# Three of four score products of a batch placed directly ahead of packed weights, in the up-projection's PSUM banks, and the second softmax done by halves of heads

## The chip, the core and the metric

The kernel runs on one core of one Trainium2 chip. The time is that of one execution in device microseconds (us). The core's engines work side by side, each through its own list of instructions in order, and wait for each other by semaphores. PE multiplies matrices (PEld is its weight load), DVE and ACT do the elementwise work and empty PSUM, POOL does a little, and SP, ACT and POOL issue DMAs. PE writes its results to PSUM, eight banks of 128 x 512 float32.

## The reference, cut to what matters

```python
def sm_attn(qq, kk, vv):                      # softmax(qq kk^T / 8) vv
    s = scale * np.matmul(qq, kk.transpose(0, 1, 3, 2))
    a = np.exp(s - np.max(s, axis=-1, keepdims=True))
    return np.matmul(a / (np.sum(a, axis=-1, keepdims=True) + 1e-09), vv)
p_packed = sm_attn(p, k, v)                   # p: (8, 8, 32, 64); q, k, v: (8, 8, 576, 64)
attn = sm_attn(q, p_packed, p_packed)         # first and second softmax
x = attn.transpose(0, 2, 1, 3).reshape(8 * 576, 512)
h = x @ w_in                                  # 512 -> 2048
out = (h * np.tanh(np.log1p(np.exp(h)))) @ w_out   # mish, 2048 -> 512
```

For each of 8 batches and 8 heads, 32 learned queries `p` gather the keys and values (first softmax), then the 576 rows of `q` read those 32 packed values (second softmax). The result goes through a two-layer network with mish between.

## The kernel before

The value product of the second attention and `w_in` are joined: for each batch the packed values of the heads are multiplied with `w_in` ("packed weights", `packed_w`, 512 of the 2048 columns at a time, chunks 0 to 3), and the second softmax's weights, turned so that heads and packs stand on the partitions (`aT_hi`, `aT_lo`), are multiplied with them. Both products of the network are done in three matmuls each, from a high and a low part of each operand.

The main loop has one step `t` for each of 8 x 16 groups; group `f` of batch `b` is 128 of the 2048 columns. A step issues on PE, in the order of the code: `down(dn, 0)`, `up(0)`, `down(dn, 1)`, `down(dn, 2)`, `up(1)`, `down(dn, 3)`. `up(0)` and `up(1)` are six matmuls each (256 and 320 columns) that write PSUM bank `ps_h0` (`ps_h` number 90 in lists) and `ps_h1` (91); ACT's mish then empties that bank (`mish`, lines 806 and 808), so `up` of the next step has to wait for it. `down(dn, c)` is three matmuls of 512 columns for one of four row chunks, of the group two steps back; `halves` (817, 818) makes its operands on DVE. Two more PSUM banks (`ps_a`) serve everything else.

Meanwhile the attention of batch `b + 1` is done in pieces between these matmuls: the generator `attention` is advanced twice a step by `advance`. It turns keys and queries on DVE (`lanes`, 450), and makes four small products on PE, by `products`: `score(0)` and `score(1)` (first softmax, heads 0 to 3 and 4 to 7) and `match(0)` and `match(1)` (second softmax). Each is eight matmuls on a quarter-wide piece of the array (64 rows by 32 columns of it, "64*32" in rows), into the two `ps_a` banks. What empties the banks is kept in `pending` and issued by `flush`: `spread` (478 to 482) after a score, `blocks` (568) after a match. `packed_w` is eight matmuls in the same 64*32 form, at the end of steps f = 2, 6, 10 and 14. The second softmax runs on both halves of the heads at once: `peak` (297, 298) on DVE, `rise` (304, the exponential) on ACT, `share`, `back`, then `upper` and `lower` make `aT_hi` and `aT_lo`.

The exponential and mish need different tables on ACT, so an exponential is preceded and followed by an ACT_TABLE_LOAD. PE's order is that of the code. On DVE and ACT a scheduler of the language sets the order of the main loop's instructions when the program is built.

Of the kernel before, what the change touches and what calls it, by code (L numbers as in the profile page):

```python
# [8 lines left out]
F32 = mybir.dt.float32  # L9
# [12 lines left out]
WB = 4  # L22
WARM = (10, 2, 3, 6, 6)
OB = 2
ATTENTION = {0: 4, 1: 0}
LOAD0 = 0
LOADS = {0: 1, 2: 1, 4: 1, 5: 1, 6: 1}
LATER = 12
# [3 lines left out]
TOGETHER = 2  # L32
# [9 lines left out]
def body(  # L42
# [12 lines left out]
    B, H, S, D = q.shape  # L55
    NP = p.shape[2]
    DF = w_in.shape[1]
    DO = w_out.shape[1]
    P = 128
# [5 lines left out]
    NF = DF // P  # L65
    HALF = S // 2
# [7 lines left out]
    att = ctx.enter_context(tc.tile_pool(name="att", bufs=2))  # L74
# [65 lines left out]
    def psum(pool, shape, name):  # L140
        return pool.tile(shape, F32, name=name, tag="acc" if pool is ps_acc else "ps_a")
# [31 lines left out]
    class Batch:  # L173
# [35 lines left out]
        def score(self, g):  # L209
            self.s_ps = scores(ps_a, self.pT[:, g, :], self.kT)  # L210
            mx = stat.tile([P, 2], F32, name="mx")
            for u in range(2):
                nc.vector.reduce_max(out=mx[:, u:u + 1], in_=self.s_ps[u], axis=AX.X)
            self.top = stat.tile([P, 1], F32, name="top")
            nc.vector.tensor_scalar(
                out=self.top, in0=mx[:, 0:1], scalar1=mx[:, 1:2], scalar2=-scale, op0=ALU.max, op1=ALU.mult
            )
# [64 lines left out]
        def match(self, g, pool):  # L282

            s2 = scores(pool, self.ppT[:, g, :], self.qT[g])
            if g == 0:
                self.a2 = moe.tile([P, 2, S // NP, NP], F32, name="a2", tag="aT_hi")
            a2f = self.a2[:, g].rearrange("a g n -> a (g n)")
            for u in range(2):
                nc.vector.transpose(out=a2f[:, u * HALF:(u + 1) * HALF], in_=s2[u])
            yield  # L290
# [84 lines left out]
    class Later(Batch):  # L375
# [78 lines left out]
                self.pinned(x)  # L454
            return t

        def products(self, packT, xT, g, paired):
            ps = [psum(ps_a, [P, HALF], f"ps_s{u}") for u in range(2)]
            for u in range(2):
                for h in range(4):  # L460
                    n = (h ^ g if paired else h) * NP
                    nc.tensor.matmul(  # L462
                        out=ps[u][h * NP:(h + 1) * NP, :],
                        lhsT=packT[u * D:(u + 1) * D, n:n + NP],
                        rhs=xT[u * D:(u + 1) * D, h ^ g, :],
                        start=True, stop=True,
                        tile_position=(u * D, h * NP),
                    )
            return ps

        def score(self, g):
            s_ps = self.products(self.pT[:, g, :], self.kT[g], g, True)
            pending.append(lambda: self.spread(g, s_ps))

        def spread(self, g, s_ps):
# [82 lines left out]
            nc.tensor.transpose(out=ps, in_=self.pp[g].rearrange("a u d -> a (u d)"), identity=ident)  # L558
            pending.append(lambda: nc.vector.tensor_copy(out=self.ppT[:, g, :], in_=ps))

        def match(self, g):
            s2 = self.products(self.ppT[:, g, :], self.qT[g], g, False)
            pending.append(lambda: self.blocks(g, s2))

        def blocks(self, g, s2):
# [2 lines left out]
                nc.vector.transpose(out=a2f[:, u * HALF:(u + 1) * HALF], in_=s2[u])  # L568

        def attention(self):  # L570


            self.by = "ACT" if self.b == 1 else None
            self.start()
            self.kT, self.qT = {}, {}
            for g in range(2):
                self.kT[g] = self.lanes(self.k_t[g])
                load_next()
                yield
            if self.b == 2:  # L580
                yield
                yield
            if self.b < TOGETHER:
                for g in range(2):
                    self.score(g)
                    yield
                    flush()
                    yield
                self.exps()
                for g in range(2):  # L590
                    self.qT[g] = self.lanes(self.q_t[g])
                    load_next()
                    yield
            else:
                self.score(0)
                yield
                flush()
                yield
                self.qT[0] = self.lanes(self.q_t[0], True)
                load_next()  # L600
                yield
                self.score(1)
                yield
                flush()
                self.qT[1] = self.lanes(self.q_t[1], True)
                load_next()
                yield
                self.exps()
                yield
                yield  # L610
            yield from self.turn_weights()
            self.sums(self.exped)
            yield
            if self.b >= TOGETHER:
                yield
                yield
            else:
                for g in range(2):
                    self.values(g)
                    yield  # L620
            for g in range(2):
                self.turned(g)
            yield
            self.a2 = att.tile([P, 2, S // NP, NP], F32, name="a2", tag="a", bufs=1)
            for g in range(2):
                self.match(g)
                yield
                flush()
                yield
            both = slice(0, 2)  # L630
            self.peak(both)
            yield
            self.rise(both)
            yield
            self.share(both)
            for g in range(2):
                self.back(g)
                yield
                self.upper(g)
                yield  # L640
                self.lower(g)

        def columns(self, a):

# [90 lines left out]
            nc.vector.tensor_tensor(out=lo[:, g], in0=ps[g], in1=hi[:, g].bitcast(F32), op=ALU.subtract)  # L735
        return [(hi[:, g], lo[:, g]) for g in range(2)]

    def packed_w(b, c):

        ps = [ps_a.tile([P, FC], F32, name=f"ps_w{g}", tag="ps_a") for g in range(2)]  # L740
        for h in range(4):
            for g in range(2):
                weave(b, ps[g].rearrange("p (u x) -> p u x", u=2), wi[c][g][:, :, h // 2], g, h)
        return [part(x) for x in ps]

    whole = {}
# [135 lines left out]
    def flush():  # L882
        while pending:
            pending.pop(0)()

    def advance(gen):
        flush()
        next(gen, None)

    def finish(gen):  # L890
        flush()
        for _ in gen:
            flush()
# [3 lines left out]
    def load_next():  # L897
        if owed["t"] < LATER and len(to_load) <= 6 * (B - 2):
            owed["n"] += 1
        elif to_load:  # L900
            b, x, g = to_load.pop(0)
            batches[b].load(x, g)
# [47 lines left out]
    with tc.manual_schedule(engines={mybir.EngineType.PE}):  # L950
# [51 lines left out]
        first.rise(slice(1, 2))  # L1002
        groups = []
        gen = iter(())
        g_rest = None
        for t in range(n_groups + LAG):
            b, f = divmod(t, NF)
            grp = None
            if t < n_groups:
                if f == 0:  # L1010
                    if b % 2 == 0:
                        g_rest = ([], [])
                if f == ATTENTION.get(b, 1) and b + 1 < B:
                    gen = batches[b + 1].attention()
                if t == LOAD0:
                    opening.close()
                    kv.append(ctx.enter_context(tc.tile_pool(name="kv", bufs=2, side="left", reuse_waits="tile")))
                owed["t"] = t
                for _ in range(LOADS.get(t, 0)):
                    load_next()  # L1020
                if t >= LATER and owed["n"]:
                    owed["n"] -= 1
                    load_next()
                if t == 1:
                    grp = ahead
                else:
                    grp = Group(b, f, None if t == 2 else wps[b, f // 4 if b else f // 2], g_rest)
                    grp.tiles()
                if t == 0:
                    ahead = Group(0, 1, wps[0, 0], g_rest)  # L1030
                    ahead.tiles()
# [24 lines left out]
                join(3)  # L1056
            if dn:
                down(dn, 0)
            if 2 < t < FLOATS:
                grp.up_floats((0,), (0, 1))  # L1060
                first.upper(t - 2)
            elif grp and t > NF:
                grp.up(0)
            if chunk:
                flush()
            else:
                advance(gen)
# [22 lines left out]
                down_rest(dn)  # L1090
            if dn:
                down(dn, 2)
            if t:
                advance(gen)
            if 2 <= t < FLOATS:
                if t == 2:
# [13 lines left out]
            if last:  # L1110
                flush()
                down_rest(dn)
            if dn:
                down(dn, 3)
            if grp and f % 4 == 2 and (b or f == NF - 2):
                nb, nch = divmod(b * (NF // 4) + f // 4 + 1, NF // 4)
                if nb < B:
                    flush()
                    if nb > b:
                        finish(gen)  # L1120
                    if f == NF // 4 + 2 and TOGETHER <= b + 1 < B:
                        batches[b + 1].both_values()
                    wps[nb, nch] = packed_w(nb, nch)
            elif b == 0 and not chunk:
                advance(gen)
# [29 lines left out]
```

## Time and profile before

| | before |
|---|---|
| median of 3 runs | 736.9 us (736.84 to 737.53) |
| span of the profiled execution | 735.2 us, 12658 instructions |
| PE busy | 724.3 us (99%) |
| DVE busy | 424.9 us (58%) |
| ACT busy | 296.6 us (40%) |
| POOL busy | 71.1 us (10%) |
| granted TensorE clock, mean | 0.999 |

The span runs from the first to the last instruction; the median of the runs is 1.7 us above it. Busy shares are means over the whole run; which wait ends last at a place is read from the rows.

### The profile page before, as it was taken

The page shows a single profiled execution, that of the slowest core. Times are in us where ns is not written, and L with a number is a line of the kernel's source. Part 1 is how long each engine was busy: PE and PEld are TensorE (multiplying, and loading weights), DVE is VectorE, ACT ScalarE, POOL GpSimd, SP SyncE. Part 2 cuts the span into 40 slices and gives each one's busy share as a digit, 9 for nine tenths or more (in the row PEclk, how much of TensorE's full clock was granted, in tenths as well). Part 3 has the DMA queues.
Part 4 walks back from the last instruction along what each step waited for, and adds up shares of the span by engine and source line. Part 5 has one row for each costly group of instructions (what it writes and reads, how often), then busy time and mean ns, then how long its engine had stood idle before and what let it go on. Part 6 is the DMA issues. An engine that isn't in the chain of part 4 may idle for free.

```text
span 735.2 us, 12658 instructions
## 1 busy us (share of the span) xinstructions
PE 724.3 (99%) x5094; PEld 553.9 (75%) x5094; DVE 424.9 (58%) x727; ACT 296.6 (40%) x692; POOL 71.1 (10%) x103
## 2 busy tenths in 40 slices
PE   9899999999999999999999999999999999999997
PEld 5455655787887878787887878877788788888885
DVE  4899887848647374546735566373833637342322
ACT  4777655534434233242522424343423424232221
POOL 1585540000000000000000000000000000000000
PEclk9999999999999999999999999999999999999999
DMA  9999972454002630144202460125101000010002
GB/s 239 297 291 231 304 121 54 94 90 96 1 37 57 116 65 1 58 73 99 33 0 72 73 121 10 44 45 100 33 1 44 30 1 1 1 58 1 1 0 72
DMA packets 187114, 56.34 MB, mean 77 GB/s; under 512 B 175024, under 2 KB 177328, under 8 KB 187056
## 3 DMA queue, kind: packets, MB, share of 16 engines
q1 hardware_dynamic: 183376, 47.14, 29.0%
q10 hardware_dynamic: 2336, 4.20, 1.5%
q0 software_dynamic: 1344, 4.20, 1.5%
q8 instruction: 40, 0.66, 0.4%
q14 instruction: 18, 0.15, 0.1%
HBM read 46.07 MB, written 9.44 MB: 75 GB/s over the span
## 4 chain that ended last, share of the span: by engine, by line
PE 92%; DVE 4%; ACT 2%; DMA 1%; issue 0%; POOL 0%; SPq 0%; DVEq 0%; ACTq 0%
PE ps_h L784 25%; PE acc L822 15%; PE acc L824 14%; PE acc L823 14%; PE acc L842 5%; PE ps_w L702 5%; PE ps_s L462 2%; PE ps_rest L824 2%; PE ps_rest L823 2%; PE ps_rest L822 2%; PE ps_h L531 1%; PE ps_h L796 1%; DMA q_n<-in_q_dram 1%; PE ps_a L511 1%; PE ps_h L909 1%; PE ps_kq L155 1%
## 5 line engine op out<-in xcount | busy, mean ns | idle before, releaser
L806 ACT ACTIVATE g<-ps_h 128x256 f32<-128x256 f32 (+2 forms) x256 | 97.0, 384 | 300.6 <-PE ps_h L784 280.4
L822 PE MATMUL acc<-wo_hi,g_hi 128*128 128x512 f32 x448 | 181.2, 405 | 0.0
L824 PE MATMUL acc<-wo_hi,g_lo 128*128 128x512 f32 x448 | 177.1, 395 | 0.0
L823 PE MATMUL acc<-wo_lo,g_hi 128*128 128x512 f32 x448 | 176.7, 394 | 0.0
L784 PE MATMUL ps_h<-aT_hi,wp_hi 128*128 128x256 f32 x496 | 153.0, 308 | 0.4 <-ACT g L806 0.4
L817 DVE CAST g_hi<-g 128x512 fp32r<-128x512 f32 x112 | 47.4, 423 | 183.4 <-ACT g L806 183.1
L784 PE MATMUL ps_h<-aT_lo,wp_hi 128*128 128x256 f32 x496 | 146.4, 295 | 0.2 <-DVE aT_lo L342 0.2
L784 PE MATMUL ps_h<-aT_hi,wp_lo 128*128 128x256 f32 x496 | 146.2, 295 | 0.0
L822 PEld LDWEIGHTS acc<-wo_hi,g_hi 128*128 128x128 f32 x448 | 84.2, 188 | 40.3 <-issue 21.3
L784 PEld LDWEIGHTS ps_h<-aT_hi,wp_hi 128*128 128x128 f32 x496 | 93.4, 188 | 15.5 <-issue 5.9
L784 PEld LDWEIGHTS ps_h<-aT_lo,wp_hi 128*128 128x128 f32 x496 | 93.4, 188 | 12.5 <-issue 3.3
L824 PEld LDWEIGHTS acc<-wo_hi,g_lo 128*128 128x128 f32 x448 | 84.1, 188 | 21.5 <-DVE g_lo L818 2.0
L784 PEld LDWEIGHTS ps_h<-aT_hi,wp_lo 128*128 128x128 f32 x496 | 93.4, 188 | 0.0
L823 PEld LDWEIGHTS acc<-wo_lo,g_hi 128*128 128x128 f32 x448 | 84.1, 188 | 9.2
L818 DVE TENSOR_TENSOR g_lo<-g,g_hi 128x512 fp32r<-128x512 f32 x112 | 77.2, 689 | 6.5 <-DVE g_hi L817 0.5
L842 PE MATMUL acc<-wo,g 128*128 128x512 f32 x128 | 61.3, 604 | 0.0
L714 DVE TENSOR_TENSOR wp_lo<-ps_w,wp_hi 128x512 fp32r<-128x512 f32 x56 | 36.1, 683 | 18.5 <-ACT wp_hi L713 18.5
L713 ACT CAST wp_hi<-ps_w 128x512 fp32r<-128x512 f32 x56 | 30.1, 591 | 37.4 <-PE ps_w L702 37.4
L851 POOL DMA_DIRECT2D out_dram<-o x16 | 9.2, 576 | 318.9 <-DVE o L831 314.7
L702 PE MATMUL ps_w<-wi,ppT 64*32 64x512 f32 (+1 forms) x576 | 37.6, 553 | 2.1 <-DVE wi L688 1.2
L842 PEld LDWEIGHTS acc<-wo,g 128*128 128x128 f32 x128 | 22.4, 189 | 22.8 <-issue 19.2
L808 ACT ACTIVATE g_rest<-ps_h 128x64 f32<-128x64 f32 x128 | 28.2, 220 | 0.0
(128 smaller groups left out, 752.0 us busy)
## 6 DMA issues: line engine op xcount, KB each, us to landing
w_st<-in_moe_w_in_dram SPq DMA_DIRECT2D x16, 512.0 KB, 8.0
w_st<-in_moe_w_out_dram SPq DMA_DIRECT2D x16, 512.0 KB, 7.4
q_n<-in_q_dram SPq DMA_DIRECT2D x56, 144.0 KB, 3.1
v_n<-in_v_dram SPq DMA_DIRECT2D x56, 128.0 KB, 2.8
k_n<-in_k_dram SPq DMA_DIRECT2D x32, 144.0 KB, 3.3
out_dram<-o ACTq DMA_DIRECT2D x14, 256.0 KB, 2.0
k_n<-in_k_dram SPq DMA_DIRECT2D x96, 32.0 KB, 2.0
out_dram<-o POOLq DMA_DIRECT2D x12, 256.0 KB, 2.4
```

Of the source, the lines that this page charges most:

```text
L702: nc.tensor.matmul(out=ps[h * NP:(h + 1) * NP, :], lhsT=ppTb[row:row + D, g, h * NP:(h + 1) * NP], rhs=w[row:row + D], start=True, stop=Tr ...
L713: nc.scalar.copy(out=hi, in_=ps)
L714: nc.vector.tensor_tensor(out=lo, in0=ps, in1=hi.bitcast(F32), op=ALU.subtract)
L784: nc.tensor.matmul(out=ps, lhsT=w[:, fs], rhs=a[:, g, cs], start=(n == 0), stop=(n == 5))
L806: nc.scalar.activation(out=self.act[:, a:a + m], in_=ps[:, :m], func=AF.Mish)
L808: nc.scalar.activation(out=self.g_rest[self.b % 2][self.f // 4][:, self.f % 4, :], in_=ps[:, m:n], func=AF.Mish)
L817: nc.vector.tensor_copy(out=hi, in_=self.act)
L818: nc.vector.tensor_tensor(out=lo, in0=self.act, in1=hi.bitcast(F32), op=ALU.subtract)
L822: nc.tensor.matmul(out=acc, lhsT=hi[:, cs], rhs=wh, start=start, stop=False)
L823: nc.tensor.matmul(out=acc, lhsT=hi[:, cs], rhs=wl, start=False, stop=False)
L824: nc.tensor.matmul(out=acc, lhsT=lo[:, cs], rhs=wh, start=False, stop=stop)
L842: nc.tensor.matmul(out=accs[c], lhsT=grp.act[:, cs], rhs=wo[f], start=f == 0, stop=f == NF - 1)
```

## The change

Nothing changes for the attention of batch 1. For batches 2 to 7 the generator is replaced by a table, `plan`, which says what is issued at which half step (`step(2 * f)` and `step(2 * f + 1)`), and three of the four small products move to the loop's own code, in `excursion`:

- at f = 2, `score(0)` of the next batch stands right ahead of `packed_w(b, 1)`; at f = 8, `match(0)` right ahead of `packed_w(b, 3)`; at f = 12, `match(1)` right ahead of `packed_w(b + 1, 0)`. They write `ps_h0` and `ps_h1` instead of `ps_a`. `score(1)` stays alone, at f = 3, in `ps_a`; `packed_w(b, 2)` stays at the end of f = 6;
- at these three steps `up(0)` moves behind `down(dn, 2)`, and `down(dn, 3)` ahead of `up(1)`;
- the second softmax runs in two halves, each after its match: `peak`, `rise`, `share`, `back`, `upper`, `lower` from f = 8 on for heads 0 to 3, from f = 12 on for heads 4 to 7.

```diff
-ATTENTION = {0: 4, 1: 0}
+ATTENTION = {0: 4}
+SOFTEN = (17, 25)
+SCORE_0, MATCH_0, MATCH_1 = 2, 8, 12
...
-        def products(self, packT, xT, g, paired):
-            ps = [psum(ps_a, [P, HALF], f"ps_s{u}") for u in range(2)]
+        def products(self, packT, xT, g, paired, beside=False):
+            if beside:
+                ps = [up_ps[u][:, :HALF] for u in range(2)]
+            else:
+                ps = [psum(ps_a, [P, HALF], f"ps_s{u}") for u in range(2)]
...
+        def plan(self):
...
+            first = 0 if self.b == TOGETHER else 2
+            steps = {
+                first: [self.start, lambda: self.keys(0)],
+                first + 1: [lambda: self.keys(1)],
+                4: [lambda: self.queries(0)],
+                7: [lambda: self.score(1)],
+                8: [lambda: self.queries(1)],
+                9: [self.exps],
+                11: [lambda: [None for _ in self.turn_weights()]],
+                12: [lambda: self.sums(self.exped)],
+                15: [lambda: self.turned(0), lambda: self.turned(1)],
+            }
+            for g, n in enumerate(SOFTEN):
+                gs = slice(g, g + 1)
+                steps[n] = [lambda gs=gs: self.peak(gs)]
+                steps[n + 1] = [lambda gs=gs: self.rise(gs)]
+                steps[n + 2] = [lambda gs=gs: self.share(gs)]
+                steps[n + 3] = [lambda g=g: self.back(g), lambda g=g: self.upper(g)]
+                steps[n + 4] = [lambda g=g: self.lower(g)]
+            return steps
...
-    def packed_w(b, c):
+    def packed_w(b, c, before=None):
+        if before:
+            before()
         ps = [ps_a.tile([P, FC], F32, name=f"ps_w{g}", tag="ps_a") for g in range(2)]
         for h in range(4):
             for g in range(2):
                 weave(b, ps[g].rearrange("p (u x) -> p u x", u=2), wi[c][g][:, :, h // 2], g, h)
+        if before:
+            flush()
         return [part(x) for x in ps]
...
+    def excursion(b, f):
+        n = batches[b + 1]
+        if f == SCORE_0:
+            wps[b, 1] = packed_w(b, 1, lambda: n.score(0, True))
+        elif f == MATCH_0:
+            wps[b, 3] = packed_w(b, 3, lambda: n.match(0, True))
+        else:
+            wps[b + 1, 0] = packed_w(b + 1, 0, lambda: n.match(1, True))
...
             if dn:
                 down(dn, 0)
+            away = grp and TOGETHER <= b + 1 < B and f in (SCORE_0, MATCH_0, MATCH_1)
+            if away:
+                flush()
+                excursion(b, f)
...
-            elif grp and t > NF:
+            elif grp and t > NF and not away:
                 grp.up(0)
...
             if dn:
                 down(dn, 2)
+            if away:
+                grp.up(0)
+                down(dn, 3)
...
-            if dn:
+            if dn and not away:
                 down(dn, 3)
```

How the built programs stand at the places of the second softmax, in the attention of batch 5 (`a_4604` is its tile of scores). On PE before, `match(1)` stood alone between `up(0)` and a `down`:

```order
L784 MATMUL ps_h_90<-aT_hi,wp_lo 128x256
L462 MATMUL ps_s_4649<-xT,ppT 32x288 x4
L462 MATMUL ps_s_4650<-xT,ppT 32x288 x4
L822 MATMUL acc_4216<-wo_hi_1917,g_hi 128x512
L823 MATMUL acc_4216<-wo_lo_1918,g_hi 128x512
```

and in the changed kernel, at f = 12, it stands between a `down` and the packed weights (lines are those of the changed file; 467 is the product, 714 the packed weights, 840 a `down`):

```order
L840 MATMUL acc_4224<-wo_hi,g_lo 128x512
L467 MATMUL ps_h_90<-xT,ppT 32x288 x4
L467 MATMUL ps_h_91<-xT,ppT 32x288 x4
L714 MATMUL ps_w_4783<-wi_0_92,ppT 32x512
L714 MATMUL ps_w_4784<-wi_1_93,ppT 32x512
```

So the product and the packed weights follow each other without a matmul of the whole array between them; `up(0)` of this step comes six `down` matmuls later.

On ACT before, the one exponential of the second softmax and its two table loads stood between the mish of `up(0)` and that of `up(1)` of one step:

```order
L806 ACTIVATE g<-ps_h_90 128x256
L304 ACT_TABLE_LOAD
L304 ACTIVATE a_4604<-a_4604 128x1152
L806 ACT_TABLE_LOAD
L806 ACTIVATE g<-ps_h_91 128x256
```

In the changed kernel the exponential of a half stands behind the casts of the packed weights and ahead of the mish of `up(0)` of its own step (306 is the exponential, 725 the cast, 822 mish):

```order
L725 CAST wp_hi<-ps_w_4783 128x512
L725 CAST wp_hi<-ps_w_4784 128x512
L306 ACT_TABLE_LOAD
L306 ACTIVATE a_4604<-a_4604 128x576
L822 ACT_TABLE_LOAD
L822 ACTIVATE g<-ps_h_90 128x256
L822 ACTIVATE g<-ps_h_91 128x256
```

So the emptying of `ps_h0` comes behind an exponential and a table load. What the exponential waits for stands on DVE in this order in the changed kernel (575 is `blocks`, 452 the next batch's keys, 299 and 300 `peak`, 726 the low part of the packed weights):

```order
L575 STREAM_TRANSPOSE a_4604<-ps_h_90 128x288
L575 STREAM_TRANSPOSE a_4604<-ps_h_91 128x288
L452 STREAM_TRANSPOSE xT<-k_n 128x1152
L299 TENSOR_REDUCE mx_4819<-a_4604 128x18
L300 TENSOR_TENSOR a_4604<-a_4604,mx_4819 128x576
L726 TENSOR_TENSOR wp_lo<-ps_w_4783,wp_hi 128x512
```

The keys of the following batch stand between `blocks` and `peak`, as they did before. These orders are the same at f = 8 and f = 12 for the attention of batches 3 to 6; for batch 7 the keys are missing (there is no batch 8), and for batch 2 the mish of `up(0)` stands ahead of the exponential, that of `up(1)` behind it. On SP and POOL the two programs have the same rows in the same order.

## Rows read from the trace of the kernel before

**Rows 1.** The page: busy us, share of the span, instructions.

```profile
PE 724.3 (99%) x5094; PEld 553.9 (75%) x5094; DVE 424.9 (58%) x727; ACT 296.6 (40%) x692; POOL 71.1 (10%) x103
```

**Rows 2.** Waits of PE: us in total, times, longest us.

```profile
PE ps_h L784 <- ACT g L806: 0.4, 1, 0.4
```

**Rows 3.** Timeline of PE, batch 2: start us, us, engine, line, operation, tiles, shape.

```profile
304.25 0.28 PE L784 MATMUL ps_h<-aT_lo,wp_hi 128*128 128x256 f32 x1
304.37 0.28 PE L784 MATMUL ps_h<-aT_hi,wp_lo 128*128 128x256 f32 x1
304.57 0.71 PE L462 MATMUL ps_s<-xT,pT 64*32 64x288 f32 x16
305.22 0.50 PE L822 MATMUL acc<-wo_hi,g_hi 128*128 128x512 f32 x1
305.56 0.40 PE L823 MATMUL acc<-wo_lo,g_hi 128*128 128x512 f32 x1
305.80 0.40 PE L824 MATMUL acc<-wo_hi,g_lo 128*128 128x512 f32 x1
...
308.41 1.09 PE L702 MATMUL ps_w<-wi,ppT 64*32 64x512 f32 x16
...
309.77 0.39 PE L823 MATMUL acc<-wo_lo,g_hi 128*128 128x512 f32 x1
...
314.04 0.40 PE L822 MATMUL acc<-wo_hi,g_hi 128*128 128x512 f32 x1
...
318.41 0.40 PE L822 MATMUL acc<-wo_hi,g_hi 128*128 128x512 f32 x1
```

**Rows 4.** Timeline of PE, opening: one 64*32 product alone, then two in sequence.

```profile
27.81 0.64 PE L702 MATMUL ps_w<-wi,ppT 64*32 64x256 f32 x8 [1.20 <-DVE wi L688]
...
37.84 1.03 PE L702 MATMUL ps_w<-wi,ppT 64*32 64x256 f32 x16
```

**Rows 5.** Timeline, all engines, around `match(1)` of the attention of batch 5.

```profile
434.78 0.72 PE L462 MATMUL ps_s<-xT,ppT 64*32 64x288 f32 x16
...
435.53 0.85 DVE L568 STREAM_TRANSPOSE a<-ps_s 128x288 f32<-128x288 f32 x2 [1.17 <-PE ps_s L462]
...
436.31 1.33 DVE L450 STREAM_TRANSPOSE xT<-k_n 128x1152 f32<-128x1152 f32 x1
...
437.56 1.31 DVE L297 TENSOR_REDUCE mx<-a 128x36 f32<-128x1152 f32 x1
```

**Rows 6.** Groups by line and shape: count | busy us, mean ns | idle before.

```profile
L713 ACT CAST wp_hi<-ps_w 128x512 fp32r<-128x512 f32 x56 | 30.1, 591 | 37.4 <-PE ps_w L702 37.4
...
L304 ACT ACT_TABLE_LOAD x7 | 9.0, 1283 | 0.1
...
L298 DVE TENSOR_TENSOR a<-a,mx 128x576 f32<-128x576 f32 x2 | 1.5, 768 | 0.1
...
L297 DVE TENSOR_REDUCE mx<-a 128x18 f32<-128x576 f32 x2 | 1.4, 722 | 0.0
L304 ACT ACTIVATE a<-a 128x576 f32<-128x576 f32 x2 | 1.4, 684 | 0.5 <-DVE a L298 0.5
```

**Rows 7.** Timeline, all engines, batch 1: mish after an exponential, and PE.

```profile
146.36 0.40 PE L824 MATMUL acc<-wo_hi,g_lo 128*128 128x512 f32 x1
146.67 0.66 ACT L806 ACTIVATE g<-ps_h 128x256 f32<-128x256 f32 x2
147.11 0.19 PEld L784 LDWEIGHTS ps_h<-aT_hi,wp_hi 128*128 128x128 f32 x1 [0.78 <-ACT g L806]
147.11 0.38 PE L784 MATMUL ps_h<-aT_hi,wp_hi 128*128 128x256 f32 x1 [0.35 <-ACT g L806]
...
147.33 0.28 PE L784 MATMUL ps_h<-aT_lo,wp_hi 128*128 128x256 f32 x1
```

**Rows 8.** Timeline of DVE: `spread` after a `score(0)` (batch 5).

```profile
397.29 0.82 DVE L478 TENSOR_REDUCE mx<-ps_s 128x1 f32<-128x288 f32 x2 [1.36 <-PE ps_s L462]
...
398.34 0.94 DVE L482 TENSOR_SCALAR a<-ps_s,top 128x288 f32<-128x288 f32 x2
```

More of the change, by code (lines that the diff above doesn't have):

```diff
@@ L469, in products, with score @@
             return ps
-        def score(self, g):
-            s_ps = self.products(self.pT[:, g, :], self.kT[g], g, True)
+        def score(self, g, beside=False):
+            s_ps = self.products(self.pT[:, g, :], self.kT[g], g, True, beside)
             pending.append(lambda: self.spread(g, s_ps))
@@ L559, in turned, with match @@
             pending.append(lambda: nc.vector.tensor_copy(out=self.ppT[:, g, :], in_=ps))
-        def match(self, g):
-            s2 = self.products(self.ppT[:, g, :], self.qT[g], g, False)
+        def match(self, g, beside=False):
+            if g == 0:
+                self.a2 = att.tile([P, 2, S // NP, NP], F32, name="a2", tag="a", bufs=1)
+            s2 = self.products(self.ppT[:, g, :], self.qT[g], g, False, beside)
             pending.append(lambda: self.blocks(g, s2))
@@ L570, in attention @@
         def attention(self):
-            self.by = "ACT" if self.b == 1 else None
+            self.by = "ACT"
             self.start()
@@ L579, in attention @@
                 yield
[L580 to L595, printed above, removed]
+            for g in range(2):
+                self.score(g)
                 yield
@@ L598, in attention @@
                 yield
-                self.qT[0] = self.lanes(self.q_t[0], True)
+            self.exps()
+            for g in range(2):
+                self.qT[g] = self.lanes(self.q_t[g])
                 load_next()
[L601 to L609, printed above, removed]
                 yield
@@ L613, in attention @@
             yield
-            if self.b >= TOGETHER:
+            for g in range(2):
+                self.values(g)
                 yield
[L616 to L620, printed above, removed]
             for g in range(2):
@@ L623, in attention @@
             yield
-            self.a2 = att.tile([P, 2, S // NP, NP], F32, name="a2", tag="a", bufs=1)
             for g in range(2):
@@ L641, in attention, with keys, queries @@
                 self.lower(g)
+        def plan(self):
+            self.by = None
+            self.kT, self.qT = {}, {}
+            first = 0 if self.b == TOGETHER else 2
[18 more added lines that the diff above has]
+            return steps
+        def keys(self, g):
+            self.kT[g] = self.lanes(self.k_t[g])
+            load_next()
+        def queries(self, g):
+            self.qT[g] = self.lanes(self.q_t[g], True)
+            load_next()
         def columns(self, a):
@@ L888, in advance, with step @@
         next(gen, None)
+    def step(n):
+        flush()
+        for x in steps.pop(n, ()):
+            x()
+    def excursion(b, f):
[6 more added lines that the diff above has]
+            wps[b + 1, 0] = packed_w(b + 1, 0, lambda: n.match(1, True))
     def finish(gen):
@@ L1004, in body @@
         gen = iter(())
+        steps = {}
         g_rest = None
@@ L1012, in body @@
                         g_rest = ([], [])
-                if f == ATTENTION.get(b, 1) and b + 1 < B:
+                if f == ATTENTION.get(b):
                     gen = batches[b + 1].attention()
+                if f == 0 and TOGETHER <= b + 1 < B:
+                    steps = batches[b + 1].plan()
                 if t == LOAD0:
@@ L1058, in body @@
                 down(dn, 0)
+            away = grp and TOGETHER <= b + 1 < B and f in (SCORE_0, MATCH_0, MATCH_1)
+            if away:
+                flush()
+                excursion(b, f)
             if 2 < t < FLOATS:
@@ L1061, in body @@
                 first.upper(t - 2)
-            elif grp and t > NF:
+            elif grp and t > NF and not away:
                 grp.up(0)
-            if chunk:
+            if b:
+                step(2 * f)
+            elif chunk:
                 flush()
@@ L1092, in body @@
                 down(dn, 2)
-            if t:
+            if away:
+                grp.up(0)
+                down(dn, 3)
+            if b:
+                step(2 * f + 1)
+            elif t:
                 advance(gen)
@@ L1116, in body @@
                 nb, nch = divmod(b * (NF // 4) + f // 4 + 1, NF // 4)
-                if nb < B:
+                if nb < B and (nb, nch) not in wps:
                     flush()
-                    if nb > b:
+                    if nb > b == 0:
                         finish(gen)
```

## The prediction

> **What bounds the kernel now.** The page comes first: PE is busy in 724.3 of 735.2 us, DVE in 58% and ACT in 40% [rows 1]. The waits say whether PE's share hides stalls: in the main loop PE waits for ACT once, for 0.4 us, before an `up` [rows 2]. So the time is what PE has to issue, and a change gains by shortening PE's own list or loses by making it wait. The timeline of PE shows what its list holds besides full matmuls. The reader should look at starts, since the ends overlap: an `up` matmul follows the one before by 0.12 us, a `down` matmul by 0.24 (305.56 to 305.80), and a whole step without extras, from one `down` matmul to the same place a step on, takes 4.37 us (314.04 to 318.41) [rows 3]. Around the small 64*32 products this rhythm breaks. The profiled execution spans 735.2 us and the median of the runs is 736.9, so 1.7 us lie around the span; the sum below is a difference and goes onto the median. About 0.2%, 1.5 us, is what a measurement of this kernel can tell from no change.
>
> **What the change removes on PE.** A `score` or `match` that stands alone starts 0.20 us after the last `up` matmul (304.37 to 304.57), 0.08 more than the rhythm; the second full matmul behind it starts 0.99 us after the product did; the first one behind it needs 0.34 to its successor (305.22 to 305.56) instead of 0.24 [rows 3]. The packed weights show the same with 512 columns for 288: 1.36 us (308.41 to 309.77) [rows 3]. The difference of 0.37 for 224 columns is 1.65 ns a column, so the 288 columns of a product cost 0.48 us and the rest of the 0.99, less the 0.24 that a `down` takes anyway, is 0.27 of fixed cost; with the 0.08 at the entry 0.35 us. Behind each other in the same form the fixed cost should be paid once. Rows for that exist in the opening: one product of 256 columns lasts 0.64, two in sequence 1.03, so the second adds 0.39, no more than its columns (0.42) [rows 4]. Bounds for one joined pair: 0.18 (only the gap at the entry and the 0.10 of the first full matmul fall away) to 0.35. I take 0.31, near the upper end because of the opening. The Trainium skill's TensorEngine Tiling, section Key Properties, says that changing the tiling mode, not just the tile, drains the engine; the gaps on either side of the 64*32 work in these rows agree with it. There are three pairs for each of six batches: 18 x 0.31 = 5.6 us (3.2 to 6.3).
>
> **What it adds.** The matmuls stay the same in number and size. On DVE and ACT the second softmax now takes each operation twice at half the elements. On DVE, `peak` on 576 elements takes 0.72 + 0.77 us; the other operations likewise cost a little more than half, an estimate of 1 us a batch by those rows, on an engine that is 58% busy [rows 1, 6]. On ACT each of six batches gets one more exponential with two more table loads of 1.28 us, 0.68 + 2.57 us, less what the shorter one saves [rows 6]. That is some 16 us more on an engine that is busy 40% of the time [rows 1], and as busy time it costs nothing. What counts is where it stands. The lists of SP and POOL are the same, so the transfers stay as they are.
>
> **The place of the exponential.** `ps_h0` and `ps_h1` are single: `up(0)` of a step can't start before mish of the step before has emptied `ps_h0`. At f = 8 and f = 12 the order on ACT now puts a half exponential and a table load ahead of that mish. Is ACT through in time? I count from the start of the product (0).
>
> PE: two products' columns and one fixed cost bring the second full matmul to 0.48 + 1.36 = 1.84; the first of it would have stood at 1.60 in the rhythm. From there to `up(0)` of the next step PE issues twelve `down` matmuls, `up(0)` and `up(1)`, exactly one step's work: 4.37. PE wants `ps_h0` at 5.97.
>
> DVE and ACT: `blocks` starts at 0.75 and the keys of the following batch at 1.53; they last 1.33, and `peak` begins at 2.78 [rows 5]. From there 0.72 + 0.77 for `peak`, 0.68 for the exponential, 1.28 for mish's table and, of the 0.66 that two overlapping mish take, an estimate of 0.38 for the first [rows 6, 7], with 0.03 us between dependent ones in such rows: 6.7. PE sees it 0.06 later (by that estimate mish is done at 147.05; the weight load starts at 147.11) [rows 7]. So PE waits from 5.97 to 6.76, 0.8 us, and the weights that it couldn't load ahead cost 0.1 more (147.11 to 147.33, 0.22 instead of 0.12) [rows 7]. The trace already has one such stall, after the exponential of the first softmax of batch 2: the `down` matmul at 146.36 is followed by `up` at 147.11, not 146.60 [rows 7]. It is the 0.4 of the waits, and its mechanism is the one that I now expect at f = 9 and f = 13.
>
> - Attention of batches 3 to 6: 8 places x 0.85 = 6.8 us. Bounds 0.5 (each of the eight links 0.04 shorter) and 1.1.
> - Batch 7 has no keys in between, but the exponential's own table load stands behind the two casts of the packed weights. These can start when the packed weights are done, some 0.1 after 1.60: 1.7 + 1.1 for two casts [rows 6] + 1.28 + 0.68 + 1.28 + 0.38 = 6.4. PE waits 0.5, with the reload 0.6: 1.2 us for two places (0 to 1.7).
> - Batch 2: mish of `up(0)` comes first, that of `up(1)` late, and more stands between `blocks` and `peak`. I take the same 0.85 at two places: 1.7 us (0 to 2.4).
> - Batch 2, f = 2: `up(0)` now stands behind `spread`, which empties the banks. In the steady batches `spread` is through 1.99 us after its start (397.29 to 399.28) [rows 8]; it starts 0.75 after the product, as `blocks` does [rows 5], so at 2.74, and PE, six `down` matmuls behind 1.60, wants the bank at 3.0. So it is covered, by 0.26 us. In batch 1's steps DVE also splits tiles of `w_out` between, each 128 x 512 like the casts, whose 0.59 [rows 6] is the nearest row. Two of them would use up the cover and add 0.9; I take 1.0 us (0 to 2).
>
> Sum: 6.8 + 1.2 + 1.7 + 1.0 - 5.6 = +5.1 us, so 736.9 + 5.1 = 742.0.
>
> A rule that speaks against halving: ScalarE: Activation LUTs, in the Trainium skill, section Table sets, advises to do all of one set before switching, at some 2.7 us a switch. The rows have 1.28 [rows 6]. With the page's price the twelve places would lose 1.4 us more each and the time would be 759 by it; I keep to the row.
>
> **Rivals.**
> - *Faster: ACT is in time.* If mish of `up(0)` is done by 5.97, only batch 2's `spread` and the gain remain: 736.9 - 5.6 + 1.0 = 732.3. It decides itself at a chain 0.8 us shorter. For it: the 576 rows come from the opening, two instructions each [rows 6]. Against: 0.8 is more than any of these rows could be off by, and the keys' 1.33 stand in the chain by the list's order.
> - *A draw.* The chain is 0.35 us shorter, or PE later, so that twelve places lose 0.45 each: 5.4 + 1.0 against 5.6, so 737.7.
> - *The joining gains little and stalls stay.* At 0.18 a pair the gain is 3.2: 744.4. The opening's rows speak against it.
> - *The up banks come free late at f = 2 too.* The cover of 0.26 us is thin: if the split of a `down` operand still runs on DVE when `score(0)` ends, `up(0)` waits. By the width of a `peak` operation on 576 elements, 0.77 [rows 6], that is 0.5 to 0.8 at five more places, and the time is up to 746. Against: the split waits for mish of the step before alone, which ACT has behind it when the product ends, so it should be over.
>
> **How the numbers follow.** Forecast as summed, 739.5 to 744, 0.65; thin cover or small gain, 744 to 746, 0.15; draw, 735.4 to 738.4, 0.10, and as much as 0.04 between it and the forecast; ACT in time, 0.06. The range, 738.2 to 744.8, leaves out the fast case, the draw and the far end of the slow ones. Slower than 738.4: 0.83; within 0.2%: 0.11; faster: 0.06.
>
> **What would show it.** Right: PE waits for ACT's mish at about 12 places of 0.5 to 0.9 us, all in the step behind f = 8 or f = 12, in the waits and in the weight load's idle time; the packed weights start about 0.54 us after the product with no gap; ACT busy rises by some 16 us. Wrong: no such waits (then the chain was mis-sized), product and packed weights costing together what they cost apart, or waits for DVE before `up(0)` at f = 2 of every batch.

## The result: slower, 743.1 us against 737.2

The changed kernel takes 743.06 us (median of 4 runs, 742.57 to 743.88) where the kernel before takes 737.21 (4 runs, 736.84 to 737.56). The ratio is 1.0079, 95% interval 1.0065 to 1.0093, so 5.85 us are lost. The profiled execution spans 741.3 us against 735.2.

The page's first lines, busy us, share of the span and instructions, answer to [rows 1]:

```profile
PE 722.1 (97%) x5094; PEld 554.3 (75%) x5094; DVE 430.0 (58%) x763; ACT 314.5 (42%) x710; POOL 71.1 (10%) x103
```

PE is busy 2.2 us less and yet the span is 6.1 longer: PE is made to wait. ACT's busy time is up by 17.9 us and DVE's by 5.1, and neither is near full. The waits of PE in the main loop (us in total, times, longest us) answer to [rows 2]:

```profile
PE ps_h L800 <- ACT g L822: 5.9, 11, 0.6
...
PE ps_h L800 <- ACT g_rest L824: 1.4, 2, 0.7
PE ps_h L800 <- DVE a L487: 1.4, 2, 1.2
```

Where there was one wait for mish there are now thirteen. They are also short of the loss: a wait counts from the end of the matmul before, and these ends are modelled and overlap the next start. The timeline shows what one costs. Here it is for PE, DVE and ACT in batch 4, from `match(0)` at f = 8 to `up(0)` of f = 9 (start us, us, then the instruction; L467 the product, L714 packed weights, L838 to L840 a `down`, L800 an `up`; rows left out are marked):

```profile
432.52 0.72 PE L467 MATMUL ps_h<-xT,ppT 64*32 64x288 f32 x16
433.03 1.06 PE L714 MATMUL ps_w<-wi,ppT 64*32 64x512 f32 x16
433.28 0.85 DVE L575 STREAM_TRANSPOSE a<-ps_h 128x288 f32<-128x288 f32 x2 [0.47 <-PE ps_h L467]
434.03 0.50 PE L838 MATMUL acc<-wo_hi,g_hi 128*128 128x512 f32 x1
434.05 1.34 DVE L452 STREAM_TRANSPOSE xT<-k_n 128x1152 f32<-128x1152 f32 x1
434.20 1.07 ACT L725 CAST wp_hi<-ps_w 128x512 fp32r<-128x512 f32 x2 [2.46 <-PE ps_w L714]
434.37 0.40 PE L839 MATMUL acc<-wo_lo,g_hi 128*128 128x512 f32 x1
...
435.29 1.28 ACT L306 ACT_TABLE_LOAD   x1
435.31 0.71 DVE L299 TENSOR_REDUCE mx<-a 128x18 f32<-128x576 f32 x1
...
436.06 0.76 DVE L300 TENSOR_TENSOR a<-a,mx 128x576 f32<-128x576 f32 x1
...
436.85 0.69 ACT L306 ACTIVATE a<-a 128x576 f32<-128x576 f32 x1 [0.27 <-DVE a L300]
...
437.55 1.28 ACT L822 ACT_TABLE_LOAD   x1
...
437.83 0.39 PE L838 MATMUL acc<-wo_hi,g_hi 128*128 128x512 f32 x1
...
438.30 0.40 PE L840 MATMUL acc<-wo_hi,g_lo 128*128 128x512 f32 x1
...
438.85 0.66 ACT L822 ACTIVATE g<-ps_h 128x256 f32<-128x256 f32 x2
...
439.28 0.39 PE L800 MATMUL ps_h<-aT_hi,wp_hi 128*128 128x256 f32 x1 [0.59 <-ACT g L822]
...
439.50 0.28 PE L800 MATMUL ps_h<-aT_lo,wp_hi 128*128 128x256 f32 x1
```

The last `down` matmul starts at 438.30 and `up(0)` would follow at 438.53; it starts at 439.28, 0.75 us late, and its second matmul comes 0.22 behind instead of 0.12. So 0.85 us are lost where the row says 0.59. ACT was through with the casts at 435.27, and did two table loads and the exponential before it came to mish.

The loss by place is read best from the length of each step: from the start of a step's first `down` matmul in the timeline to that of the next, after less before. A step without a change differs by at most 0.01. In batch 4 step 9 lasts 5.21 before (433.29 to 438.50) and 5.23 after (437.83, shown above, to 443.06), +0.02:

```profile
433.29 0.39 PE L822 MATMUL acc<-wo_hi,g_hi 128*128 128x512 f32 x1
...
438.50 0.40 PE L822 MATMUL acc<-wo_hi,g_hi 128*128 128x512 f32 x1
```

```profile
443.06 0.40 PE L838 MATMUL acc<-wo_hi,g_hi 128*128 128x512 f32 x1
```

Steps 0, 1 and 4 to 7 of batches 2 to 6 are the same; the others, in us:

| after less before | f = 2, 3 | 8 | 9 | 10, 11 | 12 | 13 | 14, 15 | sum |
|---|---|---|---|---|---|---|---|---|
| batch 1 (attention of batch 2) | +0.52 | +0.86 | +0.08 | -1.20 | +1.69 | +1.02 | -1.21 | +1.75 |
| batches 2 and 4 | -0.36 | +0.86 | +0.02 | -1.21 | +1.69 | +0.89 | -1.21 | +0.70 |
| batch 3 | -0.22 | +0.86 | +0.02 | -1.20 | +1.69 | +0.89 | -1.20 | +0.84 |
| batch 5 | +0.05 | +0.86 | +0.02 | -1.21 | +1.69 | +0.89 | -1.21 | +1.11 |
| batch 6 (attention of batch 7) | -0.36 | +0.86 | -0.23 | -1.21 | +1.69 | +0.63 | -1.21 | +0.17 |

A packed-weights step that became plain gives 1.21 (f = 10 and 11, 14 and 15), a step that lost its lone product 0.83 (f = 9), and a step that gained both costs 1.69 (f = 12): 0.83 + 1.21 - 1.69 = 0.35 us are saved by one joined pair. f = 2 and 3 of batches 2, 4 and 6, where nothing waits, show the same 0.36. At f = 9 the saved 0.83 is eaten by the stall, 0.85; at f = 13 the stall stands bare, 0.89.

The rest of the 6.0 us by which the last `down` matmul is later, 0.75, lies ahead of step f = 2 of batch 1, in the opening and not at a changed instruction.

### The profile page after: what moved, and what is told of

It is laid out like the page before. It is cut to its first block, busy times and chain, and to the rows that moved or that the text cites. A ratio compares the mean times of both kernels' runs of the same rounds, so it can differ in the third digit from the quotient of the medians.

```text
span 741.3 us, 12735 instructions
## 1 busy us (share of the span) xinstructions
PE 722.1 (97%) x5094; PEld 554.3 (75%) x5094; DVE 430.0 (58%) x763; ACT 314.5 (42%) x710; POOL 71.1 (10%) x103
## 4 chain that ended last, share of the span: by engine, by line
PE 76%; DVE 11%; ACT 6%; DMA 2%; SPq 2%; issue 2%; DVEq 0%; POOL 0%; ACTq 0%
PE ps_h L800 23%; PE acc L838 12%; PE acc L840 12%; PE acc L839 12%; PE acc L858 5%; PE ps_w L714 2%; ACT L822 2%; DVE xT L452 2%; PE ps_rest L840 2%; PE ps_rest L839 2%; PE ps_rest L838 2%; DVE a L300 1%; DMA q_t<-in_q_dram 1%; PE ps_h L467 1%; DVE mx L299 1%
## 5 line engine op out<-in xcount | busy, mean ns | idle before, releaser
L838 PE MATMUL acc<-wo_hi,g_hi 128*128 128x512 f32 x448 | 179.3, 400 | 0.0
L840 PE MATMUL acc<-wo_hi,g_lo 128*128 128x512 f32 x448 | 177.1, 395 | 0.0
L800 PE MATMUL ps_h<-aT_hi,wp_hi 128*128 128x256 f32 x496 | 154.7, 312 | 8.7 <-ACT g L822 5.9
L800 PE MATMUL ps_h<-aT_lo,wp_hi 128*128 128x256 f32 x496 | 146.5, 295 | 0.2 <-DVE aT_lo L344 0.2
L800 PE MATMUL ps_h<-aT_hi,wp_lo 128*128 128x256 f32 x496 | 146.3, 295 | 0.0
L800 PEld LDWEIGHTS ps_h<-aT_hi,wp_hi 128*128 128x128 f32 x496 | 93.5, 188 | 29.7 <-ACT g L822 10.7
L838 PEld LDWEIGHTS acc<-wo_hi,g_hi 128*128 128x128 f32 x448 | 84.3, 188 | 31.9 <-issue 16.8
L800 PEld LDWEIGHTS ps_h<-aT_lo,wp_hi 128*128 128x128 f32 x496 | 93.5, 189 | 11.8 <-issue 3.4
L840 PEld LDWEIGHTS acc<-wo_hi,g_lo 128*128 128x128 f32 x448 | 84.1, 188 | 21.4 <-DVE g_lo L834 2.0
L800 PEld LDWEIGHTS ps_h<-aT_hi,wp_lo 128*128 128x128 f32 x496 | 93.5, 189 | 0.0
L714 PE MATMUL ps_w<-wi,ppT 64*32 64x512 f32 (+1 forms) x576 | 36.9, 548 | 2.2 <-DVE wi L700 1.5
```

The lines of the kernel that those rows point to most:

```text
L714: nc.tensor.matmul(out=ps[h * NP:(h + 1) * NP, :], lhsT=ppTb[row:row + D, g, h * NP:(h + 1) * NP], rhs=w[row:row + D], start=True, stop=Tr ...
L800: nc.tensor.matmul(out=ps, lhsT=w[:, fs], rhs=a[:, g, cs], start=(n == 0), stop=(n == 5))
L838: nc.tensor.matmul(out=acc, lhsT=hi[:, cs], rhs=wh, start=start, stop=False)
L840: nc.tensor.matmul(out=acc, lhsT=lo[:, cs], rhs=wh, start=False, stop=stop)
```

## The experiments

Theory A is that of the prediction: joining saves PE one change of the array's form, and the loss comes from the exponential and mish's table load standing ahead, in ACT's list, of the mish that PE waits for. The rivals were that the waits belong to the products sitting in the `up` banks (B), that the halving costs by itself, and that the gain comes from moving the products, not from joining them (D). Each kernel was timed beside the kernel before; the first four shared one chip (before 737.13), the last three another (737.33).

### Exponential held in the order of the code

```diff
-            nc.scalar.activation(out=a2, in_=a2, func=AF.Exp, scale=scale)
+            x = nc.scalar.activation(out=a2, in_=a2, func=AF.Exp, scale=scale)
+            if self.b >= TOGETHER:
+                tc.keep_in_program_order(x)
```

> The exponentials of the second softmax (attention of batches 2 to 7) are held in the order of the code on ACT, so each stands behind mish of up(0) of the step after its product; all else as in the changed kernel. Theory A (the loss is the exponential and mish's table standing ahead of the mish that empties the up bank): the twelve waits of 0.6 to 0.8 us in the steps f = 9 and f = 13 go, about 10 us by the steps of the two traces, and what is left is the joining's gain and the wait at f = 2 of batch 1: 733 us, faster than before. Theory B (the waits come from the products occupying the up banks and up(0) coming late, wherever the exponential stands): no change, 743.

Measured: 732.39 us, ratio 0.9933 (0.9921 to 0.9945). ACT's timeline at the same place, in batch 4's step f = 9, and then PE's waits:

```profile
433.64 0.39 ACT L824 ACTIVATE g<-ps_h 128x256 f32<-128x256 f32 x1 [0.98 <-PE ps_h L802]
434.04 1.28 ACT L306 ACT_TABLE_LOAD   x1
435.33 0.69 ACT L306 ACTIVATE a<-a 128x576 f32<-128x576 f32 x1
436.04 1.28 ACT L824 ACT_TABLE_LOAD   x1
```

```profile
PE ps_h L802 <- DVE a L489: 1.2, 1, 1.2
...
PE ps_h L802 <- ACT g L824: 0.3, 1, 0.3
```

The same half exponential and the same two table loads are there (13 loads for `rise` in both kernels), but mish of `up(0)` stands ahead of them, and all waits for mish but the one that the kernel before has too are gone. By steps, f = 9 now gives -0.83 and f = 13 +0.01 in every batch, and batches 2, 4 and 6 come to -1.05 each, three times 0.35. Theory A holds, B falls: the products still go to the `up` banks and `up(0)` still comes late, as in the changed kernel.

### No table loads

```diff
-            nc.scalar.activation(out=a2, in_=a2, func=AF.Exp, scale=scale)
+            func = AF.Exp if self.b < TOGETHER else AF.Mish
+            nc.scalar.activation(out=a2, in_=a2, func=func, scale=scale)
```

> The second softmax of batches 2 to 7 uses mish in place of the exponential (so its weights are not a softmax), which takes the 24 table loads of these exponentials away and leaves every instruction otherwise in its place as far as the list allows. Theory A: the chain that ends last at f = 8 and f = 12 is shorter by a table load of 1.28 us, more than the stall of 0.8, so the waits go: about 733. Rival (DVE's keys and peak set the end, the tables are beside it): little change, 741 to 743. Theory B as for the run before: 743.

Measured: 732.04 us, ratio 0.9930 (0.9918 to 0.9942). ACT's busy time falls to 283.0 us, and the steps are those of the run before to 0.1 us, but for f = 2 of batch 1. So without table loads the early place costs nothing (here too the activation of `rise` stands ahead of the mish of `up(0)`, 430.97 and 431.56 in batch 4), and with them a later place costs nothing: it takes both. The Trainium skill's ScalarE: Activation LUTs, section Table sets, advises to batch work by set. This pair of runs bounds the advice: 732.0 without 24 loads, 732.4 with them all in another place. In these kernels the loads cost time only where PE waited for the mish behind them. Each lasts 1283 ns in every group of the profile; the 2.7 us a switch that the prediction quotes from that page is not seen, as mish follows its load within 0.02 us (437.55 + 1.28 to 438.85).

### Keys held in the order of the code

```diff
-            self.kT[g] = self.lanes(self.k_t[g])
+            self.kT[g] = self.lanes(self.k_t[g], True)
```

> The keys' transposes (attention of batches 2 to 7) are held in the order of the code on DVE, so none stands between blocks and peak at f = 8 and f = 12. Prediction's chain taken alone (DVE 1.3 us shorter, stall 0.8): the waits go, 733. Theory A with a second chain on ACT (two casts of the packed weights, the exponential's own table, exponential, mish's table, mish), as it stood in the place of the last batch without keys (0.6 us): the stalls fall from 0.87 to 0.6 in batches 3 to 6 and somewhat in batch 2, some 2 to 3 us: 740 to 741. Theory B: 743.

Measured: 741.63 us, ratio 1.0067 (1.0050 to 1.0085); 0.6 above the second of the expectations. The interval overlaps that of the changed kernel (1.0065 to 1.0093), so the steps decide and not the time. The timeline of DVE and ACT, in batch 4, at f = 8 (first row) and f = 12:

```profile
432.38 1.34 DVE L452 STREAM_TRANSPOSE xT<-k_n 128x1152 f32<-128x1152 f32 x1
...
452.55 0.75 DVE L299 TENSOR_REDUCE mx<-a 128x18 f32<-128x576 f32 x1
452.59 1.08 ACT L725 CAST wp_hi<-ps_w 128x512 fp32r<-128x512 f32 x2 [2.47 <-PE ps_w L714]
453.34 0.76 DVE L300 TENSOR_TENSOR a<-a,mx 128x576 f32<-128x576 f32 x1
453.69 1.28 ACT L306 ACT_TABLE_LOAD   x1
...
454.98 0.69 ACT L306 ACTIVATE a<-a 128x576 f32<-128x576 f32 x1
455.68 1.28 ACT L822 ACT_TABLE_LOAD   x1
456.98 0.66 ACT L822 ACTIVATE g<-ps_h 128x256 f32<-128x256 f32 x2
```

The list moved only one of the two keys' transposes away: at f = 8 it still stands between `blocks` and `peak`, and step 9 keeps its 0.85; why it did not move isn't known. At f = 12 it is gone, and the stall falls from 0.89 to 0.63, the size that batch 6 has without keys. There DVE is through at 454.10 and the exponential no longer waits for it: ACT runs casts, table, exponential, table, mish without a gap. Two chains of almost equal length led to the late mish, and 1.26 us off one of them (454.12 to 455.38 in the changed kernel) bought 0.26.

### A `down` between product and packed weights

The exponentials as in the first run, and in `packed_w` (`excursion` passes `down(dn, 1)` as `between`):

```diff
         if before:
             before()
+            between()
...
-            if dn:
+            if dn and not away:
                 down(dn, 1)
```

> As the first run, but down(dn, 1), three full matmuls, stands between the product and the packed weights at all 18 places. Theory A (the gain is the second change of the array's form saved, 0.35 us a pair by the steps of the traces): 18 x 0.35 = 6.3 us more than the first run, 739.3 if that one is 733. By the prediction's 0.31: 738.6; by its lower bound of 0.18: 736.2. Rival D (moving the products and up(0) gives the gain, whether or not they are adjacent): the same as the first run.

Measured: 737.93 us, ratio 1.0010 (1.0002 to 1.0019), 5.5 us more than the first run, 0.31 a pair. PE's timeline in batch 4, f = 8:

```profile
429.96 0.71 PE L469 MATMUL ps_h<-xT,ppT 64*32 64x288 f32 x16
430.61 0.50 PE L841 MATMUL acc<-wo_hi,g_hi 128*128 128x512 f32 x1
430.95 0.39 PE L842 MATMUL acc<-wo_lo,g_hi 128*128 128x512 f32 x1
431.18 0.40 PE L843 MATMUL acc<-wo_hi,g_lo 128*128 128x512 f32 x1
431.50 1.09 PE L716 MATMUL ps_w<-wi,ppT 64*32 64x512 f32 x16
432.52 0.50 PE L841 MATMUL acc<-wo_hi,g_hi 128*128 128x512 f32 x1
432.86 0.39 PE L842 MATMUL acc<-wo_lo,g_hi 128*128 128x512 f32 x1
```

The entry gap (431.18 to 431.50, 0.32 where `down` needs 0.24) and the slow first full matmul (0.34 to its successor) are paid twice. By steps each of the three places is 0.33 to 0.35 longer than in the first run in batches 2, 4 and 6, and batches 2, 3, 4 and 6 come to -0.03 against the kernel before: D falls, and all of the gain is the adjacency.

### Second softmax whole, products joined

```diff
-            for g, n in enumerate(SOFTEN):
-                gs = slice(g, g + 1)
-                steps[n] = [lambda gs=gs: self.peak(gs)]
...
+            n, both = SOFTEN[1], slice(0, 2)
+            steps[n] = [lambda: self.peak(both)]
+            steps[n + 1] = [lambda: self.rise(both)]
+            steps[n + 2] = [lambda: self.share(both)]
+            steps[n + 3] = [lambda: self.back(0), lambda: self.upper(0)]
+            steps[n + 4] = [lambda: self.lower(0), lambda: self.back(1), lambda: self.upper(1)]
+            steps[n + 5] = [lambda: self.lower(1)]
```

> The products stay ahead of the packed weights as in the changed kernel, but the second softmax runs on both halves at once after match(1), nothing is held in place. ACT's list then has the exponential of 1152 elements behind both mish of its step in batches 2 to 6, and ahead of the mish of up(0) in batch 7 alone. Theory A (the place in the list decides): no stalls but one of about 1.3 us in the last batch's step f = 13 (peak 1.31 + 1.35 from 1.6, exponential 1.17, table 1.28, mish 0.38, against 5.97): about 733.5. Rival (the joined places need the halves, or the second softmax is through too late for up(0) of the next batch): waits of PE for aT_hi or aT_lo at the batches' ends, 736 or more.

Measured: 734.74 us (733.33 to 735.88), ratio 0.9961 (0.9948 to 0.9975), 1.2 over the expectation. PE's waits:

```profile
PE ps_kq L157 <- DMA q_t<-in_q_dram: 1.8, 1, 1.8
...
PE ps_h L800 <- ACT g L822: 1.5, 2, 1.2
```

By steps batch 6 has +1.46 at f = 13 and no other batch has a stall there; nothing waits for `aT_hi`, and for `aT_lo` only the 0.2 us that the kernel before has too. The halves aren't needed. From step f = 2 of batch 1 on, the steps of the execution profiled sum to 3.7 us under the kernel before, which from 737.33 would be 733.7, near the expectation. What this execution lost, it lost in the opening: it was 2.1 us behind at that step, with waits for queries (1.8 us) and keys (0.7), and shortly after the wait for queries the granted clock was 0.50, from 22.0 to 25.4 us. The other five have no trace. Two of them show a mean granted clock as low as this one's 0.997 and took 735.07 and 735.88; the three with 0.998 to 1.000 took 733.33 to 734.41. That they lost in the opening too is likely but not shown.

### Second softmax by halves, products not joined

```diff
-            away = grp and TOGETHER <= b + 1 < B and f in (SCORE_0, MATCH_0, MATCH_1)
+            away = False
...
-                4: [lambda: self.queries(0)],
+                4: [lambda: self.score(0), lambda: self.queries(0)],
...
+                16: [lambda: self.match(0)],
+                24: [lambda: self.match(1)],
```

> The second softmax stays in two halves at f = 8 and f = 12, but the products stand alone behind up(0), in ps_a, and the packed weights at the end of their own steps, as in the kernel before. In ACT's list each half exponential stands behind the mish of the up(0) of its step or behind both. Theory A: 12 more exponentials and 24 table loads with no place ahead of the mish that PE waits for cost nothing on PE; a small wait of the packed weights for ps_a at f = 2, 0.2 us a batch: 737 to 738.5. Rival (the halves' 16 us more on ACT and 5 us more on DVE cost by themselves): 740 or more.

Measured: 740.52 us, ratio 1.0043 (1.0027 to 1.0059): above the range of theory A, and about what the rival gave. The waits point elsewhere than the rival:

```profile
PE ps_w L716 <- DVE a L487: 3.1, 2, 2.4
...
PE ps_h L802 <- ACT g L824: 0.3, 1, 0.3
```

There is no new wait for mish; the steps 8 to 15 together equal those of before to 0.01. All that the steps lose is lost at f = 2 and 3: 3.4 us in batch 1 and 0.3 to 0.4 in each of the others. A lone `score(0)` stands in `ps_a` in the step of these packed weights in the kernel before too. What is new stands on DVE, here in batch 2:

```profile
228.16 0.46 DVE L483 TENSOR_REDUCE mx<-ps_s 128x1 f32<-128x288 f32 x1 [1.36 <-PE ps_s L467]
228.53 1.37 DVE L452 STREAM_TRANSPOSE xT<-q_n 128x1152 f32<-128x1152 f32 x1
229.82 0.42 DVE L483 TENSOR_REDUCE mx<-ps_s 128x1 f32<-128x288 f32 x1
...
230.47 0.94 DVE L487 TENSOR_SCALAR a<-ps_s,top 128x288 f32<-128x288 f32 x2
```

The queries' transpose, issued by this edit in the same half step as `score(0)`, stands inside `spread`, which is through 3.25 us after its start (228.16 to 231.41) and not 1.99 as in [rows 8]. So `ps_a` comes free late for the packed weights. This is read from the trace; no run moved that transpose alone. The 3.4 of batch 1 are of the slowest of the five executions (742.48), where the clock adds to them:

```profile
137.21 2.38 PE L716 MATMUL ps_w<-wi,ppT 64*32 64x512 f32 x16 [2.41 <-DVE a L487]
```

At the end of this wait the granted clock fell to 0.50, 1.2 instead of 2.4 GHz, and stayed there from 137.1 to 140.5 us, and the packed weights took 2.38 us where those of batch 2 took 1.41. So the halves, with ACT busy 315.7 us, cost nothing at f = 8 and f = 12, and the run's total says little of them.

### Exponential held, and `up(0)` later

The first run's edit, and:

```diff
-                grp.up(0)
-                down(dn, 3)
+                down(dn, 3)
+                grp.up(0)
...
-            if 0 <= t - NF < NF:
+            if 0 <= t - NF < NF and t != NF + SCORE_0:
                 split_wo(t - NF)
...
+            if t == NF + SCORE_0:
+                split_wo(SCORE_0)
```

> As the first run (exponentials held in the order of the code), with down(dn, 3) ahead of up(0) at the three joined places, so that up(0) comes 0.7 us later, and with the split of w_out's third tile at the end of the step f = 2 of batch 1 instead of its start. Theory A: the waits of up(0) for spread at f = 2 (1.4 us in batch 1, some 0.4 in batch 5, 0.14 in batch 3) lose 0.7 each or go, 1.5 to 1.9 us: 730.7. Rival (these waits are not on PE's path, or come back in the up(1) that now follows at once): 732.4 or more.

Measured: 730.51 us, ratio 0.9907 (0.9893 to 0.9920), the fastest here, 6.8 us under the kernel before and 12.5 under the changed one. The wait for `spread` is down to:

```profile
PE ps_h L802 <- DVE a L489: 0.2, 1, 0.2
```

f = 2 and 3 of batches 3 and 5 now give -0.38, as the undisturbed batches do, and batch 1 -0.62. In batches 3 and 5 only the later `up(0)` can be the reason; in batch 1 the two edits are not told apart.

## Why the prediction was right

742.0 was forecast and 743.06 came, by the mechanism that was forecast, and each term can be set beside the steps. The kernel before stood 0.3 higher in its runs this time.

- **Gain of a joined pair**, 0.31 x 18 = 5.6 us: the steps give 0.35 x 18 = 6.3, the upper bound that the text gave for a pair. Taking less than the bound was wrong by the steps; by the times, 5.5 us between the first run and the fourth, it was right. The two differ by less than the fourth run's spread (736.8 to 739.0). The packed weights start 0.51 us behind the product (432.52 to 433.03), where 0.54 was forecast. The Trainium skill's TensorEngine Tiling, section Key Properties, that a change of mode drains the engine, agrees with the gaps of the fourth run, which come back with the change of form.
- **Stalls in batches 3 to 6**, 8 x 0.85 = 6.8: 0.85 at f = 9 and 0.89 at f = 13, 7.0 us. The count from the product's start holds to a few hundredths: second full matmul 1.84 forecast, 1.85 in the timeline (432.52 to 434.37); `peak` 2.78 and 2.79; PE wants the bank at 5.97 and 6.01; it gets it at 6.76 and 6.76. The mechanism is shown by the first two runs.
- **Batch 7**, 1.2: 0.60 (0.83 - 0.23) and 0.63, 1.23 us. That chain, from the casts through two table loads, is the one that the third run brought out in the other batches. The prediction's fast rival put the point of decision at a chain 0.8 us shorter; on DVE's side alone that isn't enough, since ACT's own chain is only 0.26 shorter.
- **Batch 2**, 1.7 and 1.0: 0.91 + 1.02 at f = 9 and 13, and at f = 2 0.88 net (0.52 + 0.36). PE waits 1.2 us there by the list, but in the kernel before the packed weights had a wait of 0.3 at this place that is now gone. Besides the two splits of `w_out` that the text counted, a copy of an output tile and the split of a `down` operand stand ahead of or inside `spread` on DVE there, so that 1.0 came so near is in part luck.
- **The thin cover at f = 2**, a rival, came in a small part: batch 5 loses 0.41 and batch 3 0.14, the others nothing. The last run, with 0.7 us more cover, takes both away. But what held `spread` up was not the split of a `down` operand that the rival named. It was the copy of an output tile (L847), as the timeline of DVE in batch 5 shows, where the product starts at 481.43:

```profile
482.55 0.69 DVE L847 COPY o<-acc 128x512 f32<-128x512 f32 x1 [0.64 <-DMA out_dram<-o]
483.16 0.81 DVE L483 TENSOR_REDUCE mx<-ps_h 128x1 f32<-128x288 f32 x2
```

The copy itself waited for an earlier tile's DMA, and `spread` starts 1.73 us after the product instead of 0.75. In batch 3 it starts 1.45 after, behind the same copy; in batches 2, 4 and 6 the copy is done by then.

The terms that were mis-sized most are the gain, 0.7 us too small by the steps, and this cover: 0.55 us were lost at places that the sum had at nothing. The two errors pull in opposite directions, so the closeness of the sum is in part luck. Summed from the steps, 7.0 + 1.23 + 1.93 + 0.88 + 0.55 - 6.3 = +5.3, against the forecast's +5.1 and 5.85 between the medians; the profiled opening's 0.75 is the rest of the two spans' difference.

## What to carry to other kernels

Joining work of one array form is worth its fixed cost, here 0.35 us a pair, but what the joined work feeds comes due at another time: read the consumer's list on the other engines, not only PE's. Before an engine's short job is moved, ask what stands ahead of the instruction that empties the next matmul's bank; here a table load and an exponential there cost 0.85 us a time, and nothing one instruction later. Where an order is left to a scheduler, one pinned line can be worth more than the change itself: 10.7 us here (743.06 to 732.39).

## What the runs showed that was not expected

The opening is not the same from one execution to the next: with the same instructions up to there, step f = 2 of batch 1 began between 0.4 us earlier and 2.1 us later than in the kernel before, over the eight profiled executions of the kernels behind it. PE waits there for loads and what DVE makes of them (1.8 us for `q_t` in one of them). Effects of a few tenths were for this reason read from single steps of the traces, which with few exceptions repeat to 0.01 us, and not from the totals.

TensorE's clock was not the same in all executions either. In two of the profiles the granted clock fell to 0.50 (1.2 instead of 2.4 GHz) in the midst of the kernel, each time about a wait of PE: from 22.0 to 25.4 us, where PE had waited 1.78 us until 21.2 (second softmax whole), and from 137.1 to 140.5 us, at the end of a wait of 2.41 us (halves alone). In the other seven it stayed at the upper level until the last few us. That may be behind part of the spread of the times: every execution with a mean granted clock of 0.997 or less, ten in all, is among the longest of its kernel. Eight of the ten have no trace, so for them it isn't shown.
